# Accumulating a second product in PSUM onto a copy of the first, in a chain of two feed-forward networks

## The chip, the cores and the metric

The kernel runs on one core of a Trainium2 chip. The metric is the device time of one execution in microseconds (us), the median of three runs. TensorE (PE in the profile) multiplies matrices into PSUM, which has eight banks of 128 partitions by 512 float32; PEld is its weight load. VectorE (DVE), ScalarE (ACT) and GpSimd (POOL) do the rest, and SyncE (SP) starts most DMAs.

## What is computed

```python
def reference(q, k, v, moe_w_in, moe_w_out, moe2_w_in, moe2_w_out):
    attn = _attn_ref(q, k, v)                    # retention, 4 x 8 heads, 768 steps, head size 64
    x = attn.transpose(0, 2, 1, 3).reshape(3072, 512)
    h = x @ moe_w_in                             # 512 -> 2048
    x = (h / (1 + np.exp(-1.702 * h))) @ moe_w_out   # 2048 -> 512
    h = x @ moe2_w_in
    r = np.maximum(h, 0)
    return (r * r) @ moe2_w_out
```

## The kernel before

Every float32 product is made of three matmuls of split operands (low by high, high by high, high by low), each 128 x 128 weights against 512 columns. After the retention stage, the tokens are worked off in blocks of 512 or 1024. Four of the six 512-token column blocks of the first network's up product, and two of its down product, are done plainly (lines 643 to 645, 674 to 676, 795 to 797). What is left goes through a scheme of seven products in place of eight, after Strassen: a block (l, n) is 1024 tokens of network l, cut in two halves of tokens, two halves of the inner dimension and two of the output. There are four such up stages ((0,2), (1,0), (1,1), (1,2)), each done by `up2`, and five such down stages (those and (0,1), whose up is plain), each done by `down2`.

An up stage runs over eight slices p (`NQ` = 8) of the hidden dimension. A product in it is six matmuls (`product`, line 850). Accumulators are PSUM banks taken from a first-in first-out list (`bank`, line 838). For slice p, TensorE's order, which is the order of the program, is:

- product 1 into a new bank X; ScalarE copies X into the SBUF tile g[11] (line 864 in `copy`);
- for slice p-1: product 4 onto its X, an activation from PSUM into g[21] (lines 890 to 893), product 3 onto its Z, a VectorE addition into g[12]; in slice 0 there is nothing of this;
- background work (below), if any;
- product 2 into a new bank Y; VectorE adds Y to g[11] (line 869 in `add`), and the activation of g[11] follows in SBUF: Gelu in network 0 (line 871), Relu and Square on ScalarE in block (1,0) (lines 873, 874), one VectorE instruction in (1,1) and (1,2) (line 876). ScalarE's activations are put on a list, `late`, that is emptied behind the next copy;
- product 6 onto X (X now holds 1 + 6); ScalarE copies X into g[12];
- product 5 into a new bank Z;
- product 7 onto X; ScalarE copies X into g[22], and VectorE adds Z;
- background work.

Product 6 must not write X before the copy of X into g[11] has read it, product 7 not before the copy into g[12], and product 4 not before the copy into g[22].

A down stage takes the products in the order 1, 2, 6, 5, 7, 4, 3 (`ORDER`). Each goes through four steps m, and each step through two output halves e with six matmuls each, so that the accumulator of half 0 is finished six matmuls ahead of that of half 1. At the end of each half `after` copies or adds the accumulators into SBUF tiles o (ScalarE line 978, VectorE line 981), and `store` sends them to DRAM: from POOL's queue, and in the last block from SP's for half 0 and ScalarE's for half 1. For each step, `prepare` splits a g tile into the moving operands gx: a ScalarE cast (line 946) and a VectorE subtraction (line 947); three steps' worth of gx exist at a time. In the first twelve steps VectorE also makes sums of g tiles (`sums`, lines 955 to 961), and from step 12 on the next block's operands are made (`x_operands`, lines 702 to 723).

The weights of each product are fetched from DRAM in the order of `queue`, eight ahead, on SP's queue (line 761). In blocks (0,2) and (1,0), `background` slips the making of the second network's weights between the products: ScalarE's part of it is lines 129, 130 and 383, the casts and scalings of `later`, which are issued in program order at the two calls of `background` in each slice.

Of the kernel before, what the change touches and what calls it, by code (L numbers as in the profile page):

```python
# [15 lines left out]
ACTF = mybir.ActivationFunctionType  # L16
# [4 lines left out]
B, H, S, D = 4, 8, 768, 64  # L21
# [15 lines left out]
NQ = NF // 2  # L37
# [23 lines left out]
def tile_retention_then_two_ffns(  # L61
# [10 lines left out]
    nc = tc.nc  # L72
# [368 lines left out]
    with tc.manual_schedule():  # L441
# [194 lines left out]
        acc = {}  # L636
# [98 lines left out]
        queue = deque()  # L735
        for l, n in blocks:
            first, *rest = [(i, m) for i in ORDER for m in range(NQ // 2)]
            for p in range(NQ if (l, n) == plain else 0, NQ + 1):
                if p < NQ:
                    queue.append((l, n, 0, 1, p))  # L740
                else:
                    queue.extend((l, n, 1, first[0], q) for q in range(2))
                if p > 0 and (l, n) != plain:
                    queue.extend((l, n, 0, i, p - 1) for i in (4, 3))
                if p < NQ:
                    queue.extend((l, n, 0, i, p) for i in (2, 6, 5, 7))
            for i, m in rest:
                queue.extend((l, n, 1, i, p) for p in (2 * m, 2 * m + 1))
        fetched = {}
# [34 lines left out]
        banks = deque(range(8))  # L784
# [53 lines left out]
        def bank(name):  # L838
            k = banks.popleft()
            return ps_p[0].tile([P, TB], F32, tag=f"b{k}", name=name), k  # L840
# [4 lines left out]
        def up2(l, n, first):  # L845

            xb, yb, zb = {}, {}, {}
            late = deque()

            def product(i, p, a, start):  # L850
                s, b = PRODUCT[i]
                w = fetched.pop((l, n, 0, i, p)).rearrange("p k (h c) -> p k h c", h=2)
                for k in range(2):
                    hi, lo = w[:, k, 0], w[:, k, 1]
                    matmul(a, lo, xh[b][:, k], start and k == 0, False)
                    matmul(a, hi, xh[b][:, k], False, False)
                    matmul(a, hi, xl[b][:, k], False, k == 1)
                fetch()

            def gt(q, p):  # L860
                return g[q, p // 2][:, p % 2]

            def copy(t, a):
                nc.scalar.copy(out=t, in_=a)  # L864
                while late:
                    late.popleft()()

            def add(t, a):
                v.tensor_tensor(out=t, in0=a, in1=t, op=ALU.add)  # L869
                if l == 0:  # L870
                    late.append(lambda: nc.scalar.activation(out=t, in_=t, func=ACTF.Gelu_apprx_sigmoid))
                elif n == 0:
                    late.append(lambda: nc.scalar.activation(out=t, in_=t, func=ACTF.Relu))
                    late.append(lambda: nc.scalar.activation(out=t, in_=t, func=ACTF.Square))
                else:
                    v.scalar_tensor_tensor(out=t, in0=t, scalar=0.0, in1=t, op0=ALU.max, op1=ALU.mult)

            for p in range(NQ + 1):
                if p < NQ:
                    xb[p] = bank(f"X{l}_{n}_{p}")  # L880
                    product(1, p, xb[p][0], True)
                    copy(gt(11, p), xb[p][0])
                else:
                    next(first)
                if p > 0:
                    a, k = xb.pop(p - 1)
                    product(4, p - 1, a, False)
                    t = gt(21, p - 1)
                    if l == 0:
                        nc.scalar.activation(out=t, in_=a, func=ACTF.Gelu_apprx_sigmoid)  # L890
                    else:
                        nc.scalar.activation(out=t, in_=a, func=ACTF.Relu)
                        nc.scalar.activation(out=t, in_=t, func=ACTF.Square)
                    banks.append(k)
                    a, k = zb.pop(p - 1)
                    product(3, p - 1, a, False)
                    add(gt(12, p - 1), a)
                    banks.append(k)
                    if p == NQ - 1:
                        prepare(l, n)  # L900
                if p < NQ:
                    if (l, n) != blocks[-1] and p < NQ - 1:
                        background(BGUP[l])
                    yb = bank(f"Y{l}_{n}_{p}")
                    product(2, p, yb[0], True)
                    add(gt(11, p), yb[0])
                    banks.append(yb[1])
                    product(6, p, xb[p][0], False)
                    copy(gt(12, p), xb[p][0])
                    zb[p] = bank(f"Z{l}_{n}_{p}")  # L910
                    product(5, p, zb[p][0], True)
                    product(7, p, xb[p][0], False)
                    copy(gt(22, p), xb[p][0])
                    add(gt(22, p), zb[p][0])
                    if (l, n) != blocks[-1] and p < NQ - 1:
                        background(BGUP[l])
                if p == NQ:
                    while late:
                        late.popleft()()
                if p > 1 and p % 2 == 0:  # L920
                    thirds(p // 2 - 1)
                if p == NQ - 2:
                    prepare(l, n)
# [39 lines left out]
        def down2(l, n, loads, tick):  # L963
            xb, yb, zb = {}, {}, {}
# [10 lines left out]
            def copy(q, e, a):  # L975
                if e == 0:
                    y[q] = xy_p.tile([P, 2, TB], F32, tag="xy", name=f"o{l}_{n}_{q}")
                nc.scalar.copy(out=y[q][:, e], in_=a[e][0])

            def add(q, e, a):  # L980
                v.tensor_tensor(out=y[q][:, e], in0=a[e][0], in1=y[q][:, e], op=ALU.add)  # L981
                store(q, e)

            def after(i, e, a):
                if i == 1:
                    copy(11, e, a)
                elif i == 2:
                    add(11, e, a)
                elif i == 6:
                    copy(12, e, a)  # L990
                elif i == 7:
                    copy(22, e, a)
                    add(22, e, zb)
                elif i == 4:
                    copy(21, e, a)
                    store(21, e)
                elif i == 3:
                    add(12, e, a)

            def free(a):  # L1000
                for e in range(2):
                    banks.append(a[e][1])

            for i in ORDER:
                if i in (1, 2, 5):
                    acc = {1: xb, 2: yb, 5: zb}[i]
                    for e in range(2):
                        acc[e] = bank(f"D{l}_{n}_{i}_{e}")
                else:
                    acc = zb if i == 3 else xb  # L1010
                for m in range(NQ // 2):
                    gi, gm, hi, lo = ready.popleft()
                    assert (gi, gm) == (i, m)
                    u = 4 * ORDER.index(i) + m
                    if u % 2 == 1 and u < 8:
                        loads(u // 2)
                    if u < 12:
                        sums(u)
                    else:
                        tick()  # L1020
                    if u > 0 or (l, n) != plain:
                        prepare(l, n)
                    for e in range(2):
                        a = acc[e][0]
                        for p in (2 * m, 2 * m + 1):
                            w = fetched[l, n, 1, i, p].rearrange("p j (h c) -> p j h c", h=2)
                            wh, wl = w[:, e, 0], w[:, e, 1]
                            s0, s1 = p == 0 and i in (1, 2, 5), p == NQ - 1
                            matmul(a, wl, hi[:, p % 2], s0, False)
                            matmul(a, wh, hi[:, p % 2], False, False)  # L1030
                            matmul(a, wh, lo[:, p % 2], False, s1)
                        if m == NQ // 2 - 1:
                            after(i, e, acc)
                    for p in (2 * m, 2 * m + 1):
                        del fetched[l, n, 1, i, p]
                    fetch()
                    yield
                if i == 2:
                    free(yb)
                elif i == 3:  # L1040
                    free(zb)
                elif i == 4:
                    free(xb)
# [113 lines left out]
```

## Time and profile before

| what | value |
| --- | --- |
| median of 3 runs | 1038.53 us (1037.5 to 1039.65) |
| the profiled execution, its own time | 1038.15 us |
| its span | 1036.4 us |
| TensorE busy | 1027.1 us, 99% |
| VectorE busy | 763.2 us, 74% |
| ScalarE busy | 558.6 us, 54% |

Busy time of TensorE is the time in which at least one matmul was in flight; matmuls overlap in the array, so one of 0.39 us can start every 0.23 us. "Idle before" in a row is the time that the engine did nothing just ahead of an instruction, with what released it. Times on the timeline are from the start of the span, which is 1.75 us shorter than the execution's time.

### The profile page before, as it was taken

To read this page: it belongs to the slowest core of one execution; us is meant where nothing else is said; L and a number is where in the kernel's file an instruction comes from. 1 tells how busy PE (TensorE), PEld (TensorE's weight loads), DVE (VectorE), ACT (ScalarE), POOL (GpSimd) and SP (SyncE) were. 2 spreads that over 40 slices of the span, in tenths; PEclk is the share of its full clock that TensorE was granted. 3 is DMA by queue.
4 is the path that set the end of the run, shared out by engine and by line. 5 is a ranking of instruction groups with operands and counts; after the bars stand their busy time and mean duration, and the time that the engine had idled before them with its cause. 6 is when DMAs were issued, how large, how long until landed. Compare 5 with 4: busy or idle time off the path is not lost.

```text
span 1036.4 us, 15595 instructions
## 1 busy us (share of the span) xinstructions
PE 1027.1 (99%) x5602; PEld 849.2 (82%) x5602; DVE 763.2 (74%) x1059; ACT 558.6 (54%) x906; POOL 111.2 (11%) x167
## 2 busy tenths in 40 slices
PE   8999999999999999999999999999999999999998
PEld 6888888888888888888888888888888888888886
DVE  5798998898888888467887566886445986355953
ACT  4578775344767455456555588554233464234443
POOL 2121210111333000111000111000000001000000
PEclk9999999999999999999999999999999999999999
DMA  9995898865799776999877899876776777766664
GB/s 343 398 405 182 261 312 298 316 235 219 266 339 304 262 253 219 320 343 349 279 243 226 300 373 309 263 234 227 219 195 193 258 228 228 220 194 194 208 198 163
DMA packets 114636, 274.03 MB, mean 264 GB/s; under 512 B 12160, under 2 KB 12288, under 8 KB 114304
## 3 DMA queue, kind: packets, MB, share of 16 engines
q1 hardware_dynamic: 89312, 179.71, 53.1%
q0 software_dynamic: 24672, 92.28, 25.4%
q8 instruction: 45, 0.74, 0.3%
q10 hardware_dynamic: 576, 1.05, 0.3%
q14 instruction: 31, 0.25, 0.1%
HBM read 199.59 MB, written 73.40 MB: 263 GB/s over the span
## 4 chain that ended last, share of the span: by engine, by line
PE 84%; DVE 0%; issue 0%
PE D L843 37%; PE X L843 17%; PE Z L843 8%; PE Y L843 4%; PE h L797 3%; PE h L795 3%; PE h L796 3%; PE y L676 2%; PE y L674 2%; PE y L675 2%; PE h L643 2%; PE h L645 1%; PE h L644 1%; DVE o L981 0%
## 5 line engine op out<-in xcount | busy, mean ns | idle before, releaser
L843 PE MATMUL D<-gx,r 128*128 128x512 f32 x1680 | 383.1, 389 | 0.0
L843 PEld LDWEIGHTS D<-gx,r 128*128 128x128 f32 x1680 | 315.0, 188 | 66.7 <-DVE gx L947 1.4
L947 DVE TENSOR_TENSOR gx<-g,gx 128x1024 fp32r<-128x1024 f32 x140 | 170.6, 1221 | 47.1 <-ACT gx L946 46.7
L946 ACT CAST gx<-g 128x1024 fp32r<-128x1024 f32 x140 | 145.1, 1051 | 106.1 <-PE D L843 95.0
L843 PE MATMUL X<-xh,r 128*128 128x512 f32 x512 | 157.6, 389 | 0.0
L864 ACT COPY g<-X 128x512 f32<-128x512 f32 x96 | 56.2, 585 | 154.7 <-PE X L843 154.7
L869 DVE TENSOR_TENSOR g<-Z,g 128x512 f32<-128x512 f32 x64 | 44.2, 691 | 123.0 <-ACT g L864 93.6
L843 PEld LDWEIGHTS X<-xh,r 128*128 128x128 f32 x512 | 96.0, 188 | 20.0 <-ACT g L864 0.2
L843 PE MATMUL X<-xl,r 128*128 128x512 f32 x256 | 99.6, 389 | 0.0
L843 PE MATMUL Z<-xh,r 128*128 128x512 f32 x256 | 78.8, 389 | 0.0
L843 PEld LDWEIGHTS X<-xl,r 128*128 128x128 f32 x256 | 48.1, 188 | 10.0
L843 PEld LDWEIGHTS Z<-xh,r 128*128 128x128 f32 x256 | 48.1, 188 | 10.0
L643 PE MATMUL h<-hl,w 128*128 128x512 f32 x128 | 50.2, 392 | 0.4 <-DVE w L167 0.2
L645 PE MATMUL h<-hl,w 128*128 128x512 f32 x128 | 49.8, 389 | 0.0
L644 PE MATMUL h<-hl,w 128*128 128x512 f32 x128 | 49.8, 389 | 0.0
L676 PE MATMUL y<-gl,w 128*128 128x512 f32 x128 | 49.8, 389 | 0.0
L674 PE MATMUL y<-gh,w 128*128 128x512 f32 x128 | 49.8, 389 | 0.0
L675 PE MATMUL y<-gh,w 128*128 128x512 f32 x128 | 49.8, 389 | 0.0
L795 PE MATMUL h<-hl,w 128*128 128x512 f32 x128 | 49.8, 389 | 0.0
L796 PE MATMUL h<-hl,w 128*128 128x512 f32 x128 | 49.8, 389 | 0.0
L797 PE MATMUL h<-hl,w 128*128 128x512 f32 x128 | 49.8, 389 | 0.0
L843 PE MATMUL Z<-xl,r 128*128 128x512 f32 x128 | 49.8, 389 | 0.0
(105 smaller groups left out, 1596.7 us busy)
## 6 DMA issues: line engine op xcount, KB each, us to landing
r<-kw SPq DMA_DIRECT2D x504, 256.0 KB, 3.1
kw<-wq POOLq DMA_DIRECT2D x32, 896.0 KB, 6.4
unit<-qkv SPq DMA_DIRECT2D x48, 512.0 KB, 9.2
raw<-w POOLq DMA_DIRECT2D x32, 512.0 KB, 6.2
kw<-wh POOLq DMA_DIRECT2D x16, 1024.0 KB, 4.7
kw<-w SPq DMA_DIRECT2D x16, 512.0 KB, 4.7
raw<-win POOLq DMA_DIRECT2D x16, 512.0 KB, 6.4
raw<-wout POOLq DMA_DIRECT2D x16, 512.0 KB, 7.7
```

What stands on the lines that cost most here:

```text
L643: nc.tensor.matmul(hp, lo[:, k], xh, start=(k == 0), stop=False)
L644: nc.tensor.matmul(hp, hi[:, k], xh, start=False, stop=False)
L645: nc.tensor.matmul(hp, hi[:, k], xl, start=False, stop=(k == KD - 1))
L674: nc.tensor.matmul(a, lo[:, e], gh, start=s0, stop=False)
L675: nc.tensor.matmul(a, hi[:, e], gh, start=False, stop=False)
L676: nc.tensor.matmul(a, hi[:, e], gl, start=False, stop=s1)
L795: nc.tensor.matmul(hp, lo[:, k], xh, start=(k == 0), stop=False)
L796: nc.tensor.matmul(hp, hi[:, k], xh, start=False, stop=False)
L797: nc.tensor.matmul(hp, hi[:, k], xl, start=False, stop=(k == KD - 1))
L843: nc.tensor.matmul(a, w, b, start=start, stop=stop, skip_group_check=True)
L946: nc.scalar.copy(out=hi, in_=src)
L947: v.tensor_tensor(out=lo, in0=src, in1=hi, op=ALU.subtract)
```

## The change

In an up stage, ScalarE copies X behind product 1 into the PSUM bank Y of the slice, not into g[11]. Product 2 accumulates onto it, and the activation reads Y in PSUM and writes g[11]; it is issued right behind product 2, on ScalarE, also in blocks (1,1) and (1,2). VectorE's addition of Y goes. In slice 0, where no product of a slice before lies between products 1 and 2, product 5 with its bank Z is put between them; the fetches of weights follow that order. In a down stage the same is done: ScalarE copies each half's product 1 into a second bank, product 2 accumulates onto it, and ScalarE copies the sum into o, where VectorE added it before.

```diff
-                    queue.extend((l, n, 0, i, p) for i in (2, 6, 5, 7))
+                    queue.extend((l, n, 0, i, p) for i in ((2, 6, 5, 7) if p else (5, 2, 6, 7)))
...
                     product(1, p, xb[p][0], True)
-                    copy(gt(11, p), xb[p][0])
+                    yb[p] = bank(f"Y{l}_{n}_{p}")
+                    copy(yb[p][0], xb[p][0])
...
                     if (l, n) != blocks[-1] and p < NQ - 1:
                         background(BGUP[l])
-                    yb = bank(f"Y{l}_{n}_{p}")
-                    product(2, p, yb[0], True)
-                    add(gt(11, p), yb[0])
-                    banks.append(yb[1])
+                    if p == 0:
+                        zb[p] = bank(f"Z{l}_{n}_{p}")
+                        product(5, p, zb[p][0], True)
+                    a, k = yb.pop(p)
+                    product(2, p, a, False)
+                    t = gt(11, p)
+                    if l == 0:
+                        nc.scalar.activation(out=t, in_=a, func=ACTF.Gelu_apprx_sigmoid)
+                    else:
+                        nc.scalar.activation(out=t, in_=a, func=ACTF.Relu)
+                        nc.scalar.activation(out=t, in_=t, func=ACTF.Square)
+                    banks.append(k)
                     product(6, p, xb[p][0], False)
                     copy(gt(12, p), xb[p][0])
-                    zb[p] = bank(f"Z{l}_{n}_{p}")
-                    product(5, p, zb[p][0], True)
+                    if p > 0:
+                        zb[p] = bank(f"Z{l}_{n}_{p}")
+                        product(5, p, zb[p][0], True)
                     product(7, p, xb[p][0], False)
                     copy(gt(22, p), xb[p][0])
...
             def after(i, e, a):
                 if i == 1:
+                    yb[e] = bank(f"D{l}_{n}_2_{e}")
+                    nc.scalar.copy(out=yb[e][0], in_=a[e][0])
+                elif i == 2:
                     copy(11, e, a)
-                elif i == 2:
-                    add(11, e, a)
+                    store(11, e)
...
-                if i in (1, 2, 5):
-                    acc = {1: xb, 2: yb, 5: zb}[i]
+                acc = xb if i in (1, 6, 7, 4) else yb if i == 2 else zb
+                if i in (1, 5):
                     for e in range(2):
                         acc[e] = bank(f"D{l}_{n}_{i}_{e}")
-                else:
-                    acc = zb if i == 3 else xb
...
-                            s0, s1 = p == 0 and i in (1, 2, 5), p == NQ - 1
+                            s0, s1 = p == 0 and i in (1, 5), p == NQ - 1
```

## Rows read from the trace of the kernel before

**Rows 1.** The page: busy time by engine, granted clock in 40 slices.
```profile
PE 1027.1 (99%) x5602; PEld 849.2 (82%) x5602; DVE 763.2 (74%) x1059; ACT 558.6 (54%) x906; POOL 111.2 (11%) x167
PEclk9999999999999999999999999999999999999999
```

**Rows 2.** The chain that ended last, in order of time: start us, us, what.
```profile
422.24 1.36 PE X L843 x6
423.60 1.36 PE Y L843 x6
424.96 1.36 PE X L843 x6
426.32 1.36 PE Z L843 x6
427.68 4.08 PE X L843 x18
...
653.59 73.91 PE D L843 x324
...
958.87 73.45 PE D L843 x324
```

**Rows 3.** Waits, whole span: engine, line, waited for: us in total, times, longest.
```profile
PEld D L843 <- DVE gx L947: 1.4, 5, 0.4
PEld X L843 <- ACT g L864: 0.2, 1, 0.2
ACT o L978 <- PE D L843: 34.5, 40, 6.1
```

**Rows 4.** Timeline, slice 0 of (0,2): start us, us, engine, line, what.
```profile
423.21 0.39 PE L843 MATMUL X<-xl,r 128*128 128x512 f32 x1
...
423.63 0.59 ACT L864 COPY g<-X 128x512 f32<-128x512 f32 x1 [8.69 <-PE X L843]
```

**Rows 5.** Timeline, slice 6 of (1,0): a weight load held up by a copy.
```profile
629.55 0.57 ACT L864 COPY g<-X 128x512 f32<-128x512 f32 x1
...
630.17 0.30 PEld L843 LDWEIGHTS X<-xh,r 128*128 128x128 f32 x2 [0.16 <-ACT g L864]
630.27 0.63 PE L843 MATMUL X<-xh,r 128*128 128x512 f32 x2
```

**Rows 6.** Groups of instructions by line and form: count, busy us, mean ns, idle before.
```profile
L869 DVE TENSOR_TENSOR g<-Y,g 128x512 f32<-128x512 f32 x32 | 22.0, 688 | 4.4 <-PE Y L843 4.2
L876 DVE SCALAR_TENSOR_TENSOR g<-g 128x512 f32<-128x512 f32 x48 | 33.2, 692 | 1.6
L981 DVE TENSOR_TENSOR o<-D,o 128x512 f32<-128x512 f32 x30 | 20.3, 689 | 29.2 <-PE D L843 26.9 <-ACT o L978 2.2
L978 ACT COPY o<-D 128x512 f32<-128x512 f32 x40 | 23.5, 588 | 34.5 <-PE D L843 34.5
L871 ACT ACTIVATE g<-g 128x512 f32<-128x512 f32 x24 | 14.5, 633 | 1.8 <-DVE g L869 1.8
L946 ACT CAST gx<-g 128x1024 fp32r<-128x1024 f32 x140 | 145.1, 1051 | 106.1 <-PE D L843 95.0 <-DVE gx L947 5.2 <-DVE o L981 4.2
```

**Rows 7.** Timeline of ScalarE, slice 3 of (1,0).
```profile
603.96 0.58 ACT L892 ACTIVATE g<-X 128x512 f32<-128x512 f32 x1
604.57 0.63 ACT L893 ACTIVATE g<-g 128x512 f32<-128x512 f32 x1
605.11 0.93 ACT L383 CAST wq<-w 128x896 fp32r<-128x896 f32 x1
605.94 0.68 ACT L129 ACTIVATE raw<-raw 128x512 f32<-128x512 f32 x1
606.51 0.66 ACT L130 ACTIVATE raw<-raw 128x512 uint32<-128x512 uint32 x1
607.35 0.59 ACT L864 COPY g<-X 128x512 f32<-128x512 f32 x1 [0.18 <-PE X L843]
```

**Rows 8.** The chain that ended last, slice 3 of (1,0) and slice 7 of (0,2).
```profile
490.24 1.36 PE Y L843 x6
...
608.67 3.40 PE X L843 x15
```

**Rows 9.** Timeline of ScalarE, slice 7 of (0,2): a cast ahead of the copy.
```profile
488.65 1.05 ACT L946 CAST gx<-g 128x1024 fp32r<-128x1024 f32 x1
489.59 0.59 ACT L864 COPY g<-X 128x512 f32<-128x512 f32 x1
```

**Rows 10.** Windows: stretch, its us, busy by engine with counts, granted clock, DMA share, GB/s.
```profile
40.00:110.00 70.00, 68.08 (x933) 58.26 (x926) 62.35 (x96) 52.38 (x140) 13.73 (x22) 1.00 0.83 313
574.70:653.60 78.90, 78.90 (x349) 65.24 (x348) 51.40 (x92) 63.83 (x108) 11.27 (x15) 1.00 0.96 327
```

## The prediction

> **What bounds the kernel now.** I read the page first: TensorE is busy 99% of the span and its granted clock is full in every slice [rows 1]; VectorE, from which the change takes work, is at 74%. The chain of waits says the same with more edge: in the stages that the change touches it is TensorE and nothing else. Six matmuls take 1.36 us, 0.227 us each, and each product starts where the one before it ended: 422.24, 423.60, 424.96, and so on [rows 2]. A down stage of 324 matmuls should by that pitch take 73.44 us; the tightest takes 73.45, the loosest 73.91 [rows 2]. The list of waits then gives all that TensorE lost to others in these stages: 1.4 us in five waits for VectorE's gx and 0.2 us in one wait for ScalarE's copy [rows 3]. So the question to be put to every edit is: does TensorE get a wait that it hadn't? The number of matmuls stays the same, and what another engine saves is worth at most those 1.6 us.
>
> **What goes, and what it is worth.** VectorE loses 32 additions of Y at 0.688 us, ten additions in the down stages at 0.689 us (two for each of five), and 16 of the 48 fused activations at 0.692 us: 22.0 + 6.9 + 11.1 = 40 us [rows 6]. All of that lies beside TensorE. The only way to the end is through the five gx waits. The down-stage additions removed are those of product 2, while the waits come where each stage starts or where the next block's operands begin; I give it 0 us, with 1.4 us as the bound.
>
> ScalarE gets ten more copies in the down stages (0.588 us) and 16 Relu and Square pairs in (1,1) and (1,2), some 1.2 us each: about 25 us in all, on an engine that is busy 54%. In (1,0), the fullest stage, it is busy 63.8 of 78.9 us [rows 10], and there the change only swaps activations from SBUF (0.63 us) for ones from PSUM (0.58 us) [rows 6, 7]. So the load is no bound. The order is, below.
>
> **The hand-over, measured.** TensorE's last matmul of product 1 starts at 423.21 and the copy starts at 423.63: 0.42 us from the start of the last matmul to ScalarE's start [rows 4]. A copy takes 0.59 us [rows 4, 6]. The way back is seen once: a copy ended at 629.55 + 0.57 = 630.12, the weight load held up by it began at 630.17 and its matmul at 630.27, 0.15 us after the copy's end [rows 5]. The whole round trip, start of last matmul to start of the first one allowed, is 0.42 + 0.59 + 0.15 = 1.16 us. Without a wait the next matmul starts 0.23 us after the last. So with nothing between, a bank that is copied and accumulated onto again costs 1.16 - 0.23 = 0.93 us of TensorE; with one product between (1.36 us) it costs nothing and has 0.43 us to spare.
>
> **Product 2 on the copy.** From slice 1 on, products 4 and 3 lie between products 1 and 2: 2.72 us, no wait for a ScalarE that is on time. In slice 0 product 5 covers it with the 0.43 us to spare. In the down stages half 1's six matmuls lie between the end of half 0 and product 2 on it: the same 0.43 us. That needs ScalarE to be free when the half ends, and it is: all 40 copies into o were waiting for TensorE, none the other way round [rows 3]. The accumulating copies write PSUM, which no row shows ScalarE doing. Bounds: 0.588 us as into SBUF from PSUM, or as long as a ScalarE instruction over twice the elements, 1.05 us [rows 6]. The first costs 0; the second overruns the 0.43 us by 0.03 at 14 to 24 places, 0.7 us at most. I take the first, same engine and size and source, and keep 0.7 us for the range. The Trainium skill (ScalarE: Activation LUTs, Step-by-step: what each stage is for) says that ScalarE writes PSUM faster than SBUF; no row here shows it, and by it the term would be zero too.
>
> **Product 5 moved ahead in slice 0.** This is where I expect the time to go. Product 5 lay between 6 and 7 and covered the copy of X into g[12]: the order was 6 (424.96), Z (426.32), 7 (427.68) [rows 2]. Now in slice 0 the order is 1, 5, 2, 6, 7, and product 7 accumulates onto the very bank that ScalarE has to read after product 6. Nothing lies between. The cost is the 0.93 us above, once in each of four up stages: 3.7 us. ScalarE has the activation of Y ahead of that copy: Relu and Square take 0.61 + 0.54 = 1.15 us [rows 7], start 0.42 us after product 2's last matmul starts, and so end 0.2 us before product 6's hand-over. No extra. Bounds: without any way back 0.78 us a stage, 3.1 us; with an activation's 0.63 us and twice the way back 1.12 us, 4.5 us. What product 5 itself needs, operand T1, is made during the down stage before, and its weight fetch is moved in SP's queue as the product is; I cost both at nothing.
>
> **The activations issued early.** Before, those of g[11] came behind the copy of 1 + 6; now they stand ahead of it, behind ScalarE's part of the background. In (1,0), slice 3, that background ends its turn at 606.51 + 0.57 = 607.08 [rows 7]. Then Relu and Square to 608.23, then the copy to 608.82, and product 7 may start at 608.97 where it started at 608.67 [rows 8]: 0.3 us. The other slices of (1,0) come out under 0.05 us by the same reckoning. In (0,2), slice 7, a cast of gx is ahead of the copy behind product 1, which ended at 489.59 + 0.59 = 490.18 [rows 9]; product 2 could now start at 490.33, where it started at 490.24 [rows 8]: 0.1 us. Together 0.4 us; bounds 0, if the waits before this one give ScalarE the time, and 1.2 us, if four slices of (1,0) lost what slice 3 does.
>
> The rest has one answer: ten stores of q = 11 wait for ScalarE's copy instead of VectorE's addition, on POOL's queue and, in the last block, SP's and ScalarE's; the copy is no later than the addition was, so the weight fetches behind on SP and the casts behind on ScalarE lose nothing. Banks come from a list in which six of eight are free when a slice starts; no one waits.
>
> **The sum.** 1038.15 (the profiled execution) + 3.7 + 0.4 = 1042.3 us; the median of the runs is 0.4 us above the profiled execution, so I predict 1042.4 us, +0.4%.
>
> **The rivals.**
> (a) Faster: relief of VectorE takes the place of the stall. Its place is the five gx waits, its price at most 1.4 us: 1036.8 us. It would decide only if product 7's new wait cost under 0.35 us in each stage, less than the copy alone takes. Against it: the copy is in the program and product 7 must not overwrite what it reads. Chance 0.03.
> (b) No change: the addition is taken off a path on which it never was, and the stall is partly hidden, some 0.3 us a stage: 1038.2 to 1040.4 us. It needs a round trip half as long as rows 4 and 5 show. Chance 0.07.
> (c) Slower by more: the gaps cost clock. TensorE at 1.2 GHz would take twice as long for what it does there; one slice (7 x 1.36 = 9.5 us) at the lower level behind each of the four gaps would cost 38 us: 1080 us. Against it: TensorE stood idle for 1.9 us of the 70 in the retention stage's second part, with gaps between its small matmuls, and was granted full clock [rows 10]. Chance 0.02. The Trainium skill (TensorE: Matmul & The Clock Gate, A second HAM failure mode: psum-queue depth-cycling) tells of a kernel where frequent short idling between groups made the clock swing; four gaps in 610 us are not frequent, and the trace shows no such swing.
> (d) Slower by somewhat more: copies into PSUM take 1.3 us or longer and product 2 waits for them at the 14 first places too, some 0.3 us each: +4 us, 1046.5 us. Chance 0.05.
> The forecast itself: 0.83.
>
> **The numbers.** The range holds the forecast's bounds: low, 3.1 us with 0.7 of (a)'s relief and no early activations, 1040.6; high, 4.5 + 0.7 + 0.7 on 1038.5, 1044.4. A measurement of this kernel can tell about 0.2%, 2.1 us, from no change. Faster by more than that 0.02, as (a) reaches 1036.8 only; within 0.08; slower 0.90.
>
> **What would show it.** Right: in the profile of after, one wait of TensorE (weight load X) for ScalarE's g, some 0.9 us idle, in slice 0 of each of four up stages, so four in all; the span of these stages 1 us longer, that of the down stages the same; VectorE's busy time 40 us less; the copies into PSUM near 0.59 us. Wrong: a wait of D for the copies into the second bank, which would make (d); a granted clock under 1.00; or product 7 starting 0.23 us after product 6 ended its issue.

## The result and the profile after

The changed kernel takes 1043.7 us (median of six runs, 1042.45 to 1046.59) against 1037.9 us for the kernel before on the same chip: 1.0058 times as long, 95% interval 1.0046 to 1.0071. It is slower by a little over half a per cent, inside the range that was given. The profiled execution took 1043.36 us, its span is 1041.5 us.

The first thing to look at is the page of the changed kernel: busy time by engine and the granted clock.

```profile
PE 1029.1 (99%) x5602; PEld 848.3 (81%) x5602; DVE 725.2 (70%) x1001; ACT 584.7 (56%) x948; POOL 111.7 (11%) x167
PEclk9999999999999999999999999999999999999999
```

VectorE lost 38 us of work and ScalarE gained 26, near the 40 and 25 that were reckoned, and the kernel became slower. TensorE has the same 5602 matmuls and its full clock in every slice of the page. So neither work nor clock explains the time. What is new stands in the waits of the weight load and of the matmuls (engine, line, waited for: us in total, times, longest):

```profile
PEld X L843 <- ACT g L864: 5.8, 9, 1.1
PEld D L843 <- DVE gx L957: 1.4, 5, 0.4
PEld Y L843 <- ACT Y L864: 0.4, 1, 0.4
PE X L843 <- ACT g L864: 2.7, 4, 0.7
```

Before, X waited once for a copy, 0.2 us [rows 3]; now nine times, and the four that idle the matmuls too are the long ones. The wait for gx, the only one that VectorE's relief could have shortened, is still 1.4 us in five. One of the four long waits, from the timeline of slice 0 of (0,2):

```profile
427.55 0.39 PE L843 MATMUL X<-xl,r 128*128 128x512 f32 x1
427.97 0.59 ACT L864 COPY g<-X 128x512 f32<-128x512 f32 x1 [0.76 <-PE X L843]
428.61 0.30 PEld L843 LDWEIGHTS X<-xh,r 128*128 128x128 f32 x2 [1.10 <-ACT g L864]
428.61 0.73 PE L843 MATMUL X<-xh,r 128*128 128x512 f32 x2 [0.68 <-ACT g L864]
```

The last matmul of product 6 starts at 427.55, ScalarE's copy 0.42 us later, and it ends at 428.56. Only then does product 7 load its weights, at 428.61. The pair of matmuls that starts there takes 0.73 us where an undisturbed pair takes 0.62: the first one's weights weren't loaded while it waited. So far that is 427.55 to 428.61, less the 0.23 us at which matmuls follow each other, plus this 0.11: 0.94 us. The matmuls behind the pair also come a little late: the sixth one after 427.55 starts at 429.88 in the timeline, 2.33 us later where six take 1.36. The whole loss is 0.97 us.

The chain of waits gives the price by stage. First three rows of the kernel before that were not shown yet (where down stages begin), then the same places after, with slice 0 of (0,2):

```profile
345.96 76.27 PE D L843 x336
501.12 73.55 PE D L843 x324
806.38 73.61 PE D L843 x324
```

```profile
346.17 76.33 PE D L843 x336
422.50 1.36 PE X L843 x6
423.86 1.36 PE Z L843 x6
425.22 1.36 PE Y L843 x6
426.58 1.37 PE X L843 x6
428.61 4.38 PE X L843 x18
...
502.64 73.55 PE D L843 x324
...
656.80 5.89 PE D L843 x26
...
730.70 1.36 PE X L843 x6
...
810.55 73.57 PE D L843 x324
...
884.12 1.36 PE X L843 x6
...
963.98 73.45 PE D L843 x324
```

The row of slice 0's product 7 begins at 428.61, not at 426.58 + 1.37 = 427.95. The last up stage takes 963.98 - 884.12 = 79.86 us; before, 958.87 [rows 2] less 806.38 + 73.61 is 78.88: 0.98 longer. That of (1,1), where there is no background either, is 0.97 longer (79.85, against 806.38 less 653.59 + 73.91 [rows 2]). The two stages with background work are longer by more: (0,2) takes 502.64 - 422.50 = 80.14 us for 78.88, 1.26 longer, and (1,0), which begins at 576.20 in the chain, takes 656.80 - 576.20 = 80.60 us for 78.92, 1.68 longer. So each stage has lost about 0.97 us, and (0,2) and (1,0) some 0.29 and 0.71 us besides. The down stages take what they took: 73.55, 73.57, 73.45.

From the beginning of the first down stage to the end of the last, the chain of waits runs 345.96 to 958.87 + 73.45 = 1032.32 before, 686.36 us, and 346.17 to 1037.43 after, 691.26 us: **4.90 us longer**. Everything that the change touches lies in this stretch, and its length hardly depends on what happens ahead of it, so the experiments are compared by it. (The expectations below count it to the start of the last matmul, 0.24 us less for every kernel.) The medians differ by 5.8 us, 0.9 us more: three of the six runs of the changed kernel show a mean granted clock of 0.998 and took 1044.0 to 1046.6 us, where the three with 1.000 took 1042.5 to 1043.4; the kernel before has such runs too (one at 0.997, 1040.84 us), and why the changed one has more of them is open.

### The profile page after: what moved, and what is told of

Read it like the earlier page. It is cut to its first block, busy times and chain, and to the rows that moved or that the text cites. A ratio compares the mean times of both kernels' runs of the same rounds, so it can differ in the third digit from the quotient of the medians.

```text
span 1041.5 us, 15565 instructions
## 1 busy us (share of the span) xinstructions
PE 1029.1 (99%) x5602; PEld 848.3 (81%) x5602; DVE 725.2 (70%) x1001; ACT 584.7 (56%) x948; POOL 111.7 (11%) x167
## 4 chain that ended last, share of the span: by engine, by line
PE 83%; ACT 1%; DVE 0%; issue 0%
PE D L843 37%; PE X L843 17%; PE Z L843 8%; PE Y L843 4%; PE h L797 3%; PE h L795 3%; PE h L796 3%; PE y L676 2%; PE y L674 2%; PE y L675 2%; PE h L643 2%; PE h L645 1%; PE h L644 1%; ACT g L864 0%; DVE g L836 0%; ACT wq L383 0%
## 5 line engine op out<-in xcount | busy, mean ns | idle before, releaser
L864 ACT COPY g<-X 128x512 f32<-128x512 f32 x64 | 37.6, 587 | 60.5 <-PE X L843 58.6
```

## The experiments

Theory S is that of the prediction: TensorE stands still where product 7 follows product 6 directly, because both use the bank that ScalarE has to copy in between. Rival P: accumulating onto a bank that ScalarE has written is itself what costs. Rival C: gaps make the clock fall. Each ratio is to runs of the kernel before beside it on the same chip; the stretch is read from one trace of each kernel.

| kernel | first down stage starts | last one ends | stretch, us | over before | median, us | ratio to before (95%) |
| --- | --- | --- | --- | --- | --- | --- |
| before | 345.96 | 1032.32 | 686.36 | | | |
| changed | 346.17 | 1037.43 | 691.26 | +4.90 | 1043.7 | 1.0058 (1.0046 to 1.0071) |
| order_only | 345.46 | 1035.77 | 690.31 | +3.95 | 1042.35 | 1.0044 (1.0031 to 1.0057) |
| slice0_as_before | 345.96 | 1033.38 | 687.42 | +1.06 | 1040.47 | 1.0024 (1.0014 to 1.0034) |
| filler | 345.86 | 1033.41 | 687.55 | +1.19 | 1039.27 | 1.0007 (0.9998 to 1.0016) |
| every_slice | 346.72 | 1064.18 | 717.46 | +31.10 | 1068.78 | 1.0297 (1.0283 to 1.0312) |
| copy_twice | 347.02 | 1040.71 | 693.69 | +7.33 | 1045.67 | 1.0074 (1.0061 to 1.0087) |
| down_only | 345.49 | 1031.82 | 686.33 | -0.03 | 1038.04 | 1.0001 (0.9992 to 1.0009) |
| filler_late | 345.75 | 1033.21 | 687.46 | +1.10 | 1039.03 | 1.0010 (1.0001 to 1.0018) |
| slice0_longer | 346.08 | 1033.68 | 687.60 | +1.24 | 1039.23 | 1.0011 (1.0002 to 1.0020) |
| slice0_late | 346.59 | 1033.16 | 686.57 | +0.21 | 1038.29 | 1.0001 (0.9992 to 1.0010) |

**The order alone.** The kernel before, with product 5 moved ahead in slice 0 and nothing else.

```diff
-                    queue.extend((l, n, 0, i, p) for i in (2, 6, 5, 7))
+                    queue.extend((l, n, 0, i, p) for i in ((2, 6, 5, 7) if p else (5, 2, 6, 7)))
...
+                    if p == 0:
+                        zb[p] = bank(f"Z{l}_{n}_{p}")
+                        product(5, p, zb[p][0], True)
                     yb = bank(f"Y{l}_{n}_{p}")
...
-                    zb[p] = bank(f"Z{l}_{n}_{p}")
-                    product(5, p, zb[p][0], True)
+                    if p > 0:
+                        zb[p] = bank(f"Z{l}_{n}_{p}")
+                        product(5, p, zb[p][0], True)
```

> The kernel before with product 5 moved ahead of product 2 in slice 0 of the four up stages, and nothing else: product 2 still goes into a bank of its own, VectorE adds it. Theory S (TensorE stands still in slice 0 between products 6 and 7, because 7 accumulates onto the bank that ScalarE is copying; 0.95 us in the profile of after): the whole of this part appears, 4 x 0.95 = 3.8 us, +0.37% on before, with four waits of X for ScalarE's copy in the profile and no others. Rival P (accumulating onto banks that ScalarE has written is what costs): no such bank here, so before's time within 0.1%. Rival C (the gaps make the clock fall now and then): the time of single runs scatters by 2 to 3 us and the granted clock of the late ones is under 1.000.

The stretch grew by 3.95 us, the time by 0.44%. Its waits of X's weight load for ScalarE:

```profile
PEld X L843 <- ACT g L864: 4.6, 5, 1.1
```

Four long ones, and the short one that was there before. No bank here is written by ScalarE and accumulated onto, so P falls as the explanation of four fifths of the loss.

**The rest without the order.** The changed kernel with slice 0 put back.

```diff
-                    yb[p] = bank(f"Y{l}_{n}_{p}")
-                    copy(yb[p][0], xb[p][0])
+                    if p == 0:
+                        copy(gt(11, p), xb[p][0])
+                    else:
+                        yb[p] = bank(f"Y{l}_{n}_{p}")
+                        copy(yb[p][0], xb[p][0])
...
-                    if p == 0:
-                        zb[p] = bank(f"Z{l}_{n}_{p}")
-                        product(5, p, zb[p][0], True)
-                    a, k = yb.pop(p)
-                    product(2, p, a, False)
+                    a, k = bank(f"Y{l}_{n}_{p}") if p == 0 else yb.pop(p)
+                    product(2, p, a, p == 0)
                     t = gt(11, p)
-                    if l == 0:
+                    if p == 0:
+                        add(t, a)
+                    elif l == 0:
```

> The changed kernel with slice 0 of the up stages as before: order 1, 2, 6, 5, 7, product 2 into a bank of its own, VectorE adds it. Slices 1 to 7 and the down stages accumulate onto the copy. Theory S: the four waits go, 3.8 us of the change; what is left is the waits behind activations issued early in (1,0) and a cast ahead of the copy in (0,2), 0.9 us by the profile of after: +0.09% on before. Rival P: 28 of 32 accumulations are still there, so at least seven eighths of +0.58% stay, +0.5%. Rival C: as S, and no run with a clock under 1.000.

The stretch came down to +1.06 us: the two parts, 3.95 and 1.06, add up to 5.01, near the 4.90 of the whole. Of the waits of X the four long ones are gone and five short ones are left:

```profile
PEld X L843 <- ACT g L864: 1.4, 5, 0.5
```

But the time was 0.24% over before, where 0.09% was expected. The other 1.1 us lie behind the last matmul; the run slice0_longer below is about them.

**All accumulations, each copy covered.** Slice 1's product 1 goes between slice 0's products 6 and 7, and its product 2 between 7 and 4.

```diff
+                if p == 0:
+                    queue.extend((l, n, 0, i, q) for i, q in ((1, 0), (5, 0), (2, 0), (6, 0), (1, 1), (7, 0)))
+                    continue
+                if p == 1:
+                    queue.extend((l, n, 0, i, q) for i, q in ((2, 1), (4, 0), (3, 0), (6, 1), (5, 1), (7, 1)))
+                    continue
...
+                if p == 1:
+                    product2(1)
+                elif p < NQ:
+                    product1(p)
...
                     copy(gt(12, p), xb[p][0])
+                    if p == 0:
+                        product1(1)
```

> The changed kernel with slice 1's product 1 put between products 6 and 7 of slice 0, and slice 1's product 2 between slice 0's 7 and 4 (order 1, 5, 2, 6, 1', 7, 2', 4, 3, 6', 5', 7'): all 32 accumulations onto the copy stay, and each copy has 1.36 us of other matmuls behind it. Theory S: the four waits of 0.95 us are gone, 0.9 us is left as above: +0.09% on before. Rival P: all of the cost stays, +0.58%. Rival C: as S, with no run under a clock of 1.000.

All 32 accumulations are there, and 3.7 of the 4.9 us are gone: +1.19 us in the stretch, 1.0007 in time with 1 inside the interval. The chain of waits at slice 0 of (0,2), products 1, 5, 2, then 6, 1' and 7 in one row, then 2':

```profile
422.16 1.36 PE X L849 x6
423.52 1.36 PE Z L849 x6
424.88 1.36 PE Y L849 x6
426.24 4.08 PE X L849 x18
430.32 1.36 PE Y L849 x6
```

No gap: 1.36 us of other matmuls behind a copy is enough. P can then explain at most the 1.19 us that are left; slice0_late, below, takes these away with 28 of the 32 accumulations in place.

**More gaps.** Product 5 moved ahead in every slice.

```diff
-                    queue.extend((l, n, 0, i, p) for i in ((2, 6, 5, 7) if p else (5, 2, 6, 7)))
+                    queue.extend((l, n, 0, i, p) for i in (5, 2, 6, 7))
...
-                    if p == 0:
-                        zb[p] = bank(f"Z{l}_{n}_{p}")
-                        product(5, p, zb[p][0], True)
+                    zb[p] = bank(f"Z{l}_{n}_{p}")
+                    product(5, p, zb[p][0], True)
...
-                    if p > 0:
-                        zb[p] = bank(f"Z{l}_{n}_{p}")
-                        product(5, p, zb[p][0], True)
                     product(7, p, xb[p][0], False)
```

> The changed kernel with product 5 moved ahead of product 2 in all eight slices, not in slice 0 alone: 32 places where 7 follows 6. Theory S: 28 more waits of 0.95 us, 26.6 us above the changed kernel, 1070 us, +3.1% on before; somewhat less in (1,0) and (0,2), if ScalarE's other waits there fall together with these. Rival P: no more accumulations than in the changed kernel, so 1043.7 us. Rival C: the clock falls far more often with eight times the gaps; each stretch at 1.2 GHz doubles the 0.227 us of a matmul in it, so the time lies clearly above 1070 us, and the granted clock well under 0.998.

```profile
PEld X L843 <- ACT g L864: 35.1, 32, 1.1
```

32 waits, 26.2 us more than the changed kernel, 0.94 us for each of the 28 added. That is a mean: the short waits of the changed kernel, some 1.0 us in all, are no longer in the list, so an added wait costs (26.2 + 1.0) / 28 = 0.97 us, as in slice 0. The granted clock was 0.999 or 1.000 in each of its four runs, with eight times the gaps, and so it was in the nine runs of order_only and copy_twice, which have four gaps as the changed kernel has. C falls. The Trainium skill (TensorE: Matmul & The Clock Gate, A second HAM failure mode: psum-queue depth-cycling) tells of short idling that makes the clock swing; 32 gaps of somewhat under 1 us in 717 us did not.

**A dearer copy.** The changed kernel with the copy into g[12] issued twice in slice 0.

```diff
                     copy(gt(12, p), xb[p][0])
+                    if p == 0:
+                        nc.scalar.copy(out=gt(12, p), in_=xb[p][0])
```

> The changed kernel with the copy of X into g[12] issued twice in slice 0 of each up stage: the suspected cost made larger. Theory S: the second copy starts 0.49 us behind the first, so each of the four waits is 0.49 us longer, 1.44 us for 0.95, and the stretch from the first down stage to the last matmul grows from 691.0 to 693.0 us. A rival in which the wait hangs on something else than the copy (the weight fetch that was moved, T1, the order of banks): the four waits stay at 0.95 us.

The waits follow the copy: +2.43 us, 0.61 for each of four; the rival, by which they would have stayed, falls. The size was missed: the second copy started 0.62 us behind the first, not 0.49, as the timeline of ScalarE in slice 0 of (0,2) shows. It writes the tile that the first one writes, and came after the first had ended.

```profile
428.83 0.58 ACT L864 COPY g<-X 128x512 f32<-128x512 f32 x1 [0.76 <-PE X L843]
429.45 0.58 ACT L920 COPY g<-X 128x512 f32<-128x512 f32 x1
```

**The down stages alone.** The kernel before with the changed `after` and accumulators of `down2`.

```diff
                 if i == 1:
+                    yb[e] = bank(f"D{l}_{n}_2_{e}")
+                    nc.scalar.copy(out=yb[e][0], in_=a[e][0])
+                elif i == 2:
                     copy(11, e, a)
-                elif i == 2:
-                    add(11, e, a)
+                    store(11, e)
```

> The kernel before with the change in the down stages alone: product 2 accumulates onto ScalarE's copy of product 1, ten copies, up stages as before. Theory S: half 1's six matmuls lie behind each copy, no new wait of TensorE, the stretch from the first down stage to the last matmul stays at 686.1 us, the time within 0.1% of before. Rival P (accumulating onto a bank that ScalarE has written costs by itself): 10 of 42 such banks, a quarter of the +0.58%, +0.14%, with longer matmul starts behind the copies. Rival (relief of VectorE pays): up to 0.9 us less.

Stretch -0.03 us, time 1.0001. Groups of its copies into PSUM and into SBUF (count, busy us, mean ns, idle before):

```profile
L987 ACT COPY D<-D 128x512 f32<-128x512 f32 x10 | 5.7, 570 | 12.4 <-PE D L843 12.4
L978 ACT COPY o<-D 128x512 f32<-128x512 f32 x40 | 23.5, 588 | 28.7 <-PE D L843 28.7
```

All the time ahead of the copies was spent waiting for TensorE, and six matmuls lie behind each: no new wait, and no gain from ten VectorE additions less.

**What is left, the early activations.** Two runs. The first is the filler kernel with the activations of g[11] put on the list `late`, so that they follow the copy into g[12], as before the change.

```diff
-                if l == 0:
-                    nc.scalar.activation(out=t, in_=a, func=ACTF.Gelu_apprx_sigmoid)
...
-                banks.append(k)
+                def act():
+                    if l == 0:
+                        nc.scalar.activation(out=t, in_=a, func=ACTF.Gelu_apprx_sigmoid)
...
+                    banks.append(k)
+
+                late.append(act)
```

> The kernel with slice 1's product 1 between slice 0's 6 and 7, and with it the activations of g[11] issued behind the copy of 1 + 6 in every slice, as the kernel before had them. Theory S: of the 1.0 us that the filler kernel still lost from the first down stage to the last matmul, the 0.74 us of waits in (1,0) go, and the 0.27 us in slice 7 of (0,2), where a cast of gx stands ahead of the copy, stays: that stretch is 686.4 us against 686.12 before, and the time within 0.1% of before. Rival (the early activations are not what holds product 7 up in (1,0)): the waits in (1,0) stay and the stretch is 687.2 us or more.

The stretch stayed at +1.10: a miss. The waits in the later slices of (1,0) went, but a new one of 1.0 us came in slice 1. ScalarE's timeline there:

```profile
588.44 0.59 ACT L870 COPY g<-X 128x512 f32<-128x512 f32 x1 [1.46 <-PE X L849]
588.93 0.63 ACT L879 ACTIVATE g<-g 128x512 f32<-128x512 f32 x1
589.59 0.63 ACT L880 ACTIVATE g<-g 128x512 f32<-128x512 f32 x1
590.13 0.58 ACT L899 ACTIVATE g<-Y 128x512 f32<-128x512 f32 x1
590.74 0.63 ACT L900 ACTIVATE g<-g 128x512 f32<-128x512 f32 x1
591.28 0.61 ACT L879 ACTIVATE g<-g 128x512 f32<-128x512 f32 x1
591.93 0.63 ACT L880 ACTIVATE g<-g 128x512 f32<-128x512 f32 x1
592.46 0.57 ACT L870 COPY g<-X 128x512 f32<-128x512 f32 x1
```

Three pairs of Relu and Square stand between the copies into g[12] and g[22], because slice 1's products 1 and 2 had been moved into slice 0, so that no copy lay between the three; slice 1's product 4 waited for the second copy. So this run mixed two things. The second makes the same edit where slice 0 is as before and nothing is moved (it stands on slice0_longer, below):

```diff
                     if p == 0:
                         add(t, a)
-                    elif l == 0:
-                        nc.scalar.activation(out=t, in_=a, func=ACTF.Gelu_apprx_sigmoid)
...
+                        banks.append(k)
+                    else:
+                        def act(t=t, a=a, k=k):
...
+                        late.append(act)
```

> The kernel with slice 0 as before and the 12 tiny instructions, and with it the activations of g[11] in slices 1 to 7 issued behind the copy of 1 + 6, where the kernel before had them. It settles what filler_late left mixed: there the waits in slices 3 to 6 of (1,0) went, but one of 0.87 us came in slice 1, where three pairs of Relu and Square came to stand ahead of the copy into g[22], since slice 1's product 2 had been moved. Here nothing is moved. Theory S: the waits of X for ScalarE's copies in (1,0) go, 0.75 us less than slice0_longer; only slice 7 of (0,2) keeps its 0.27 us; the stretch from the first down stage to the last matmul is 686.4 to 686.6 us, the time within 0.1% of before. Rival (the order of the activations is not what holds product 7 up): the stretch stays at 687.4 us.

Stretch +0.21 us, 1.03 less than with the early activations, and its list of waits has none of X for a copy any more. So the place of g[11]'s activations ahead of the copy cost most of this; 0.75 was expected, and some 0.2 of the 1.03 is not the edit's: slice0_longer's down stage of (1,1) took 73.79 us and this one's 73.57, as a weight load there waited 0.3 us for a DMA. Against slice0_as_before, which has no such wait, the stretch is 0.85 us shorter. With 28 of 32 accumulations and all of the down stages changed, this kernel is as fast as before (1.0001, 0.9992 to 1.0010), not faster.

**The end of slice0_as_before.** The kernel slice0_longer is that one with 12 small instructions more on VectorE and on ScalarE each, some 690 us before the end.

```diff
+            for i in range(12):
+                v.memset(pad[:, 0:8], 0.0)
+                nc.scalar.copy(out=pad[:, 16:24], in_=pad[:, 8:16])
             thirds(NQ // 2 - 1)
```

> The kernel with slice 0 as before took 2.1 us more than before where 0.9 us was expected; its stretch of TensorE was 1.06 us longer, as it should be, but its last store took 3.1 us from issue to landing where that of the others takes 2.0, with a 32nd packet on the queue of instructions (q14) inside it, where the others have 31. This kernel adds 12 tiny instructions each to VectorE and ScalarE at the end of the plain up stage and changes nothing else. Theory (an instruction fetch that falls into the last store): the fetch moves off the end, the last store lands in 2.0 to 2.1 us, and the time falls by 1.1 us to 1039.4 us, +0.1% on before. Rival (chance, or something else at the end): 1040.5 us as it was, last store 3.1 us.

The DMA queues and issues from the last down stage's end on, first of slice0_as_before, then of slice0_longer (issues: tiles, queue, operation, count, KB each, us from issue to landing; q14 is a queue that fetches instructions, here one packet):

```profile
q14 instruction: 1, 0.01, 0.3%
...
out<-o ACTq DMA_DIRECT2D x1, 256.0 KB, 3.1
```

```profile
out<-o ACTq DMA_DIRECT2D x1, 256.0 KB, 2.1
```

With the instructions added, no fetch falls behind the last matmul, the last store lands in 2.1 us instead of 3.1, and the median falls from 1040.47 to 1039.23 us, though the stretch is 0.18 us longer. Both kernels fetch 32 packets on q14 in all (0.26 MB, 8 KB each); in the first, one of them falls into the last store. The 1.1 us that slice0_as_before takes beyond what its stretch explains go with this fetch; how one fetch of 8 KB holds a store of 256 KB up for 1 us was not shown.

## Why the prediction was right, and where its sizes were off

**The bound.** Right: only a new wait of TensorE could count. VectorE's 38 us are worth nothing; the five gx waits stayed at 1.4 us.

**The hand-over and product 5.** Right in place, number and size: 0.93 us and four times were forecast; 0.97 us by the timeline and by the stages, 3.95 us for the order alone. The way out was the 0.42 us read from [rows 4]. The way back, put at 0.15 us, came near by luck, as [rows 5] does not measure it. The matmul there started at 630.27 because the one before it, at 630.04 in the timeline of the kernel before, had started 0.23 us earlier; it would have started then without the wait of its weights as well. In the hand-over load and matmul both start 0.05 us after the copy's end, and 0.14 us are lost behind that, since the weights could not be loaded ahead: 0.42 + 0.59 + 0.05 + 0.14 - 0.23 = 0.97.

**Product 2 on the copy.** Right: 0.576 us for a copy into PSUM in the up stages and 0.570 in the down stages, against 0.587 and 0.589 into SBUF. The Trainium skill (ScalarE: Activation LUTs, Step-by-step: what each stage is for) states that direction, and these rows agree, by 0.01 to 0.02 us. ScalarE's groups of the changed kernel:

```profile
L864 ACT COPY g<-X 128x512 f32<-128x512 f32 x64 | 37.6, 587 | 60.5 <-PE X L843 58.6
L864 ACT COPY Y<-X 128x512 f32<-128x512 f32 x32 | 18.4, 576 | 45.6 <-PE X L843 45.6
L997 ACT COPY D<-D 128x512 f32<-128x512 f32 x10 | 5.7, 570 | 12.4 <-PE D L843 12.4
```

**The early activations.** Right in mechanism, too small in size: 0.4 us was forecast for them and the cast in slice 7 of (0,2) together; slice0_as_before shows 1.06, of which 0.21 stay in slice0_late, where the one wait left is that in slice 7. The step that failed is a comparison of two clocks. I set the end of a ScalarE instruction, from the timeline, against the start of a product in the chain of waits. But a piece of the chain begins where the one before it was done, not where its first matmul starts: product 2 of slice 0 begins at 423.60 in the chain [rows 2], while the last matmul of product 1 starts at 423.21 [rows 4], so that the next one starts 0.23 later, at 423.44. The deadlines that I used for slice 3 of (1,0) and slice 7 of (0,2) were 0.16 us too late. In slice 7 the reckoned 0.1 us becomes 0.26, and the timeline of the changed kernel has it so:

```profile
489.90 1.04 ACT L956 CAST gx<-g 128x1024 fp32r<-128x1024 f32 x1
490.83 0.58 ACT L864 COPY Y<-X 128x512 f32<-128x512 f32 x1
...
491.08 0.39 PE L843 MATMUL Z<-xl,r 128*128 128x512 f32 x1
...
491.47 0.30 PEld L843 LDWEIGHTS Y<-xh,r 128*128 128x128 f32 x2 [0.42 <-ACT Y L864]
491.47 0.73 PE L843 MATMUL Y<-xh,r 128*128 128x512 f32 x2
```

From 491.08 to 491.47, less 0.23, plus the 0.11 us of the longer pair: 0.27 us. In (1,0), 0.3 us was forecast for slice 3 and under 0.05 us for each of the others. The pieces that begin with product 7 in slices 3, 4 and 5, which take 4.08 us without a wait [rows 2], are in the chain of the changed kernel:

```profile
611.38 4.38 PE X L843 x18
...
621.20 4.18 PE X L843 x18
...
630.82 4.18 PE X L843 x18
```

By the timeline slice 3 loses 0.39 us: the last matmul of product 5 starts at 610.90 and the first of product 7 at 611.38, 0.25 us late, and loses 0.14 more behind its start, as in the hand-over. Slices 2, 4 and 5 lose 0.10 to 0.12 us each and slice 7 0.03. In these the first matmul starts on time or nearly so, but its weights were held up by the copy, and the first pair takes up to 0.71 us. Together that is 0.74 us, less 0.04 that the kernel before lost to the wait of [rows 5], and it agrees with the 0.71 of the stage. In the hand-over itself all times are from the timeline, so its size held.

**The sum.** 3.7 + 0.4 were forecast for the stretch, 3.9 + 1.0 measured. The rest up to the 5.8 us between the medians is not of the stretch. The working has two slips: 1042.3 with 0.4 us added is 1042.7, not 1042.4; and the high end of the range adds 0.7 us twice, once for copies into PSUM, which leaves 0.7 us for the early activations, where their bound had been put at 1.2 and they cost 1.0. That the time came inside all the same is owed in part to luck: the 0.7 us for copies into PSUM did not come, the hand-overs took 0.6 us less than their bound, and the kernel before took 1037.9 us beside the changed one, 0.6 less than the 1038.5 that the forecast stands on.

**The rivals.** Relief of VectorE (a) and a hidden stall (b) would have shown less than four long waits. For the clock (c), every_slice is the answer. Of copies into PSUM so slow that product 2 waits at 14 places (d), there is one wait, 0.4 us, and it hangs on the cast ahead of the copy.

## What to carry to other kernels

When an accumulator is read out and then accumulated onto again, count the round trip (here 1.06 us from the last matmul's start to the next one's, and 0.97 us lost with the slow restart) and keep at least one product on another bank between. Filling one such hole with work taken from another place can open a hole there, as product 5 did here: look at what the moved work was covering. In the filler kernel an order was found that covers every copy. On a kernel that TensorE bounds without gaps, taking 38 us from VectorE is worth nothing by itself, and an instruction put earlier on ScalarE delays the copies behind it.

## What the runs showed that was not expected

After each longer wait TensorE's first pair of matmuls takes 0.73 us instead of 0.62: a stall costs 0.11 us more than the gap in the matmuls shows, 0.14 with the matmuls behind, and a weight load that is held up costs some 0.1 us even where no gap shows. And the end of a kernel can hang on its instruction count: with one 8 KB fetch inside it the last store landed 1.0 us later, and 12 more instructions on each of two engines took this away. Which engine's instructions were fetched was not settled.
